# One slot size for the rest of a routed expert layer, and the count of slots read ahead of the last slot's work

## The chip, the core and the metric

The kernel runs on one core of a Trainium2 chip. Its engines are TensorE (PE in the profile; PEld is its weight load), VectorE (DVE), ScalarE (ACT), GpSimd (POOL) and SyncE (SP, which issues most DMAs). A name with a q behind it (POOLq) is that engine's sequencer. The metric is the device time of one execution in microseconds.

## What is computed

Attention of 8 batches and 8 heads over 576 positions of 64 values, in which every score below the row's maximum less tau is dropped; then a layer of 8 experts, in which each of the 4608 tokens goes to the one expert with the highest gate.

```python
def _attn_ref(q, k, v, tau):
    scores = np.matmul(q, k.transpose(0, 1, 3, 2)) / np.sqrt(q.shape[-1])
    thresh = np.max(scores, axis=-1, keepdims=True) - tau
    scores = np.where(scores >= thresh, scores, -1000000000.0)
    attn = np.exp(scores - np.max(scores, axis=-1, keepdims=True))
    return np.matmul(attn / (np.sum(attn, axis=-1, keepdims=True) + 1e-09), v)

def _moe_ref(x, modality_id, w_gate, modality_bias, w1, w2):   # x: 4608 x 512
    logits = x @ w_gate + modality_bias[modality_id]           # 8 experts
    e_idx = np.argmax(logits, axis=1)
    probs = np.exp(logits - logits.max(-1, keepdims=True))
    gate_w = (probs / (probs.sum(-1, keepdims=True) + 1e-09))[np.arange(N), e_idx]
    for e in range(E):
        mask = e_idx == e
        out[mask] = gate_w[mask, None] * (np.maximum(x[mask] @ w1[e], 0.0) @ w2[e])
    return out
```

## The kernel before

The attention runs in 288 steps, one tile of 128 rows of scores each. Every matrix is held as a high and a low part (names that end in h and l), and a product is three matmuls, so TensorE works nearly without a pause.

The expert layer is worked in **slots**: a slot is one expert and up to 512 rows of tokens (`slot`). Each token's row number and gate weight is scattered into a DRAM table `tab` (line 683), sorted by expert; the table is first filled with a row number that no token has (`fill`, line 259). A slot reads which expert it is (`expert`, line 795) and where its rows lie in the table (`rows`, line 799) into SP's registers, loads that piece of the table (`tb`, line 801) and its weights (lines 838 and 842), gathers the tokens' rows `xg` with an indirect DMA on POOL (line 814), transposes them on TensorE (line 828) into `xh` and `xl`, multiplies by w1 (line 874, result through `hh` on ACT, line 885, and `hl` on DVE, line 886) and by w2 (line 901), adds up the two halves (`y0` on ACT, line 909; `y` on DVE, line 914), and scatters the finished rows to the output with an indirect DMA on POOL (line 916). Weights are split into high parts on ACT (line 856) and low parts on POOL or DVE (line 860).

Seven **side slots** (256, 384, 512, 512, 512, 448 and 512 rows) are worked among the attention's steps. What is then left is planned once by `pick_rest`, a run of small operations on one partition of DVE that ends in the table `si` (the experts, the row offsets, and the number of slots). Before the change it plans with three slot sizes, 512, 384 and 256 rows. Three **tail slots** of 512 rows always follow (`ALWAYS`). Behind them stand conditional slots, for routings that need more: `ask` (line 1126) reads one number, `more_i`, into a register of every engine, and each engine tests it (line 1211) and jumps over the conditional code where it is zero. In the profiled execution it is: there are 37 gathers and 37 scatters of 128 rows, 25 of the side slots and 12 of the three tail slots.

An order written by hand by due times (`at`) sets when each piece is put into the program. Within the attention's steps PE and POOL keep it; the rest is placed by the scheduler. Instructions with the same issue order token (`tc.stamp_issue_order_token`) keep the order among themselves.

## Time and profile before

| | us |
|---|---|
| runs | 1012.5, 1012.56, 1022.66 (median 1012.56) |
| the profiled execution | 1011.88 |
| its span, first to last record | 1010.2 |
| PE busy in the span | 986.6 (98%) |
| DVE, ACT, POOL busy | 681.3, 633.5, 524.8 |
| mean granted clock of TensorE | 0.998 |

The profiled execution is a run of its own, beside the three timed ones; 1.68 us of its time lie outside the span. Times in a trace count from the span's start. "Busy" leaves out what only a sequencer does (register reads, branches, semaphores, DMA issues). A chain of waits is followed back from the last instruction, at each step to what released it; "issue" in it is time for which no releaser shows.

### The profile page before, as it was taken

How to read it: one execution, taken by the hardware profiler on the slowest of the kernel's cores; microseconds unless marked ns; L12 is line 12 of the kernel's file. 1: busy time of each engine (PE TensorE's matmuls, PEld its weight loads, DVE VectorE, ACT ScalarE, POOL GpSimd, SP SyncE). 2: the span in 40 equal slices, each digit the busy share in tenths (PEclk: the TensorE clock that was granted, in tenths of full speed). 3: DMA queues.
4: the chain of work that ended last, by engine and by line, in shares of the span. 5: the costliest groups of instructions: out<-in, count | busy, mean ns of one | idle time of the engine just before them, and what ended most of it. 6: DMA issues, size and time to landing. Idle time of an engine off the chain costs nothing.

```text
span 1010.2 us, 20293 instructions
## 1 busy us (share of the span) xinstructions
PE 986.6 (98%) x6556; PEld 795.0 (79%) x6556; DVE 681.3 (67%) x1698; ACT 633.5 (63%) x1439; POOL 524.8 (52%) x728
## 2 busy tenths in 40 slices
PE   7999999999999999999999999999999999999996
PEld 6777777788888887788778888788878867888885
DVE  6888987778677766777677877777766764333422
ACT  6787887676676666666667666666667625334430
POOL 4363467377538553655455654646567274534311
PEclk9999999999999999999999999999999999999999
DMA  6667777679647665676647555667666227634301
GB/s 154 145 158 169 137 196 196 169 161 237 170 124 168 187 159 133 144 184 163 165 112 177 153 158 133 152 160 197 153 150 165 82 81 200 204 108 139 116 10 44
DMA packets 206803, 151.83 MB, mean 150 GB/s; under 512 B 100062, under 2 KB 167646, under 8 KB 206688
## 3 DMA queue, kind: packets, MB, share of 16 engines
q1 hardware_dynamic: 199488, 131.53, 53.0%
q0 software_dynamic: 7200, 18.92, 5.9%
q8 instruction: 54, 0.88, 0.4%
q14 instruction: 61, 0.50, 0.2%
HBM read 80.05 MB, written 19.48 MB: 99 GB/s over the span
## 4 chain that ended last, share of the span: by engine, by line
PE 74%; DVE 9%; issue 9%; DMA 2%; ACT 2%; POOL 2%; SPq 1%; POOLq 0%; DVEq 0%; ACTq 0%
PE bk L521 15%; PE s L402 14%; PE bk L487 10%; PE bk L901 10%; PE bk L874 10%; PE pm L901 4%; PE pm L874 3%; DVE pr L459 2%; DVE nm L435 2%; PE bk L339 2%; PE bk L828 2%; PE bk L512 1%; PE bk L573 1%; ACT e L445 1%; DMA xg<-xs,tb 1%
## 5 line engine op out<-in xcount | busy, mean ns | idle before, releaser
L435 DVE TENSOR_REDUCE nm<-s 128x1 f32<-128x576 f32 x254 | 190.9, 752 | 97.4 <-PE s L402 95.3
L459 DVE SCALAR_TENSOR_TENSOR pr<-s,nm,e 128x576 f32<-128x576 f32 x254 | 204.8, 815 | 62.7 <-ACT e L445 58.9
L445 ACT ACTIVATE e<-s,nm 128x576 f32<-128x576 f32 x254 | 188.6, 743 | 59.5 <-DVE nm L435 52.6
L402 PE MATMUL s<-km,q 128*128 128x288 f32 x1024 | 196.5, 313 | 7.5 <-DVE pr L459 6.4
L497 ACT COPY ptm<-bk 128x512 f32<-128x512 f32 x256 | 149.4, 584 | 53.2 <-PE bk L487 52.6
L487 PE MATMUL bk<-ident,pr 128*128 128x128 f32 x1152 | 173.8, 273 | 0.0
L402 PEld LDWEIGHTS s<-km,q 128*128 128x128 f32 x1024 | 146.3, 189 | 24.5 <-DVE pr L459 18.2
L487 PEld LDWEIGHTS bk<-ident,pr 128*128 128x128 f32 x1152 | 140.6, 140 | 27.3 <-issue 6.2
L521 PE MATMUL bk<-ptm,v_m 128*64 128x320 f32 (+1 forms) x1024 | 140.7, 412 | 0.3 <-DVE hl L886 0.3
L860 POOL TENSOR_TENSOR w2l<-raw,w2h 128x512 fp32r<-128x512 f32 x77 | 98.5, 1287 | 32.6 <-ACT w2h L856 28.6
L521 PEld LDWEIGHTS bk<-ptm,v_m 128*64 128x64 f32 x1024 | 68.2, 136 | 50.8 <-issue 7.9
L916 POOL DMA_INDIRECT out_dram<-y,tb x37 | 38.0, 1026 | 122.2 <-DVE y L914 92.2
L476 ACT COPY rp<-pr 128x64 f32<-128x64 f32 x271 | 60.0, 248 | 43.8 <-DVE pr L459 41.5
L874 PE MATMUL bk<-xh,w1h 128*128 128x512 f32 (+3 forms) x204 | 82.1, 402 | 0.1
L313 POOL CAST nk<-str 128x64 fp32r<-128x64 f32 x31 | 7.4, 240 | 138.3 <-ACT str L327 130.9
L874 PE MATMUL bk<-xl,w1h 128*128 128x512 f32 (+3 forms) x204 | 74.2, 363 | 0.0
L874 PE MATMUL bk<-xh,w1l 128*128 128x512 f32 (+3 forms) x204 | 74.1, 363 | 0.0
L901 PE MATMUL bk<-w2h,hh 128*128 128x512 f32 x168 | 73.4, 437 | 0.0
L860 POOL TENSOR_TENSOR w1l<-raw,w1h 128x512 fp32r<-128x512 f32 x53 | 68.1, 1285 | 4.2
L901 PE MATMUL bk<-w2h,hl 128*128 128x512 f32 x168 | 66.2, 394 | 0.0
L901 PE MATMUL bk<-w2l,hh 128*128 128x512 f32 x168 | 66.1, 393 | 0.0
L814 POOL DMA_INDIRECT xg<-xs,tb x37 | 39.0, 1053 | 38.4 <-DMA tb<-tab 16.5
(211 smaller groups left out, 1973.6 us busy)
## 6 DMA issues: line engine op xcount, KB each, us to landing
raw<-in_moe_w_dram SPq DMA_DIRECT2D x160, 256.0 KB, 3.5
q<-nq SPq DMA_DIRECT2D x124, 256.0 KB, 4.4
km<-nk SPq DMA_DIRECT2D x124, 144.0 KB, 2.5
v_m<-in_v_dram SPq DMA_DIRECT2D x32, 256.0 KB, 3.7
xs<-xr SPq DMA_DIRECT2D x32, 256.0 KB, 3.0
k_m<-in_k_dram SPq DMA_DIRECT2D x62, 128.0 KB, 3.2
q_m<-in_q_dram SPq DMA_DIRECT2D x62, 128.0 KB, 3.7
vr<-in_v_dram SPq DMA_DIRECT2D x64, 16.0 KB, 4.1
```

Of the source, the lines that this page charges most:

```text
L402: nc.tensor.matmul(out=sps[:, hf, 0:SH], lhsT=a, rhs=x, start=(z == 0), stop=(z == len(passes) - 1))
L435: in_line(nc.vector.tensor_reduce(out=nm[:, 0:1], in_=sv, axis=AX.XY, op=ALU.max, negate=True), two)
L445: in_line(nc.scalar.activation(out=e, in_=sv, func=AF.Exp, bias=nm[:, 0:1]), two and n < LEAD)
L459: in_line(nc.vector.scalar_tensor_tensor(out=pr.rearrange("p (a x) -> p a x", a=2), in0=s2[n % 2][:, :, 0:SH], scalar=th, in1=e, op0=ALU.i ...
L476: (nc.gpsimd.tensor_copy if 2 <= n < 46 else nc.scalar.copy)(out=state[("rp", p)][:, 2 * c + s + x, :], in_=pr[:, SA:S])
L487: nc.tensor.transpose(out=ps[:, kc * P:(kc + 1) * P], in_=pr[:, kc * P:(kc + 1) * P], identity=ident)
L497: in_line(nc.scalar.copy(out=ptm[:, s, :, (c % 2) * P:(c % 2 + 1) * P], in_=pv), n + 2 < LEAD)
L521: nc.tensor.matmul(out=o, lhsT=lhsT, rhs=rhs, start=start, stop=stop, skip_group_check=True)
L814: nc.gpsimd.indirect_dma_start(out=xg, out_offset=None, in_=xs[0:nrow, :], in_offset=bass.IndirectOffsetOnAxis(ap=box["tb"][:, t, 0:1].bit ...
L860: then(eng.tensor_tensor(out=lo, in0=raw, in1=hi.bitcast(F32), op=ALU.subtract), eng is nc.vector and (lined or late))
L874: nc.tensor.matmul(out=ps[:, 0:WT], lhsT=a[:, cs], rhs=x[:, c, :], start=(c == 0 and z == 0), stop=(c == KC - 1 and z == 2))
L901: nc.tensor.matmul(out=ps, lhsT=h[:, ts], rhs=w, start=(z == 0 and y == 0), stop=(z == F2 - 1 and y == 2))
```

## The change

It has five parts.

1. `pick_rest` plans with one slot size, 512 rows. The arrays with a dimension of three sizes lose it, the list of possible slots grows from 10 to 16, and `more_f`, `more_s`, `more_i` and `cnt` are gone. `si` holds the count of slots in its last place.
2. The table gets one more 512-row stretch for each expert (`TROWS` 37888 to 41984), and its fill is two DMAs from one tile of half the size.
3. In a slot whose last tile has 64 rows (the 448-row side slot), the gather, `y0`, `y` and the scatter touch 64 partitions.
4. `ask` reads the count from `si`, and its reads, one per engine, carry a token "asked", as do the first operations of the last always-run slot on each engine (`ends`): each engine's read then stands ahead of those.
5. After the last slot there is a nest of tests of that register (`more`), and no copy `done_y`.

```diff
-    CAP = -(-N // W) * W
-    NCH = CAP // W
+    NCH = -(-N // W)
+    CAP = (NCH + 1) * W
     TROWS = NE * CAP + 2 * W
...
-    MAXN = ((N - NE * (WM + 1)) // W + NE if N >= NE * (WM + 1) else N // (WM + 1),
...
-    ALWAYS = (-(-left_ // W), 0, 0)
-    MAXC = max(MAXN)
...
+    WR = W
+    MAXC = (N - NE) // WR + NE
+    ALWAYS = -(-max(W, N - sum(w for w, _ in SIDE)) // W)
...
                                         in1=mid_f[:, m, :].unsqueeze(2).to_broadcast(shp), op=ALU.mult)
             nc.gpsimd.tensor_tensor(out=bias_t, in0=bias_t, in1=bias_u, op=ALU.add)
 
-        fill = work.tile([P, TROWS // P, 2], I32, name="fill", tag="xr", bufs=2)
+        half = TROWS // P // 2
+        fill = work.tile([P, half, 2], I32, name="fill", tag="xr", bufs=2)
         nc.gpsimd.memset(fill[:, :, 0], N)
         nc.gpsimd.memset(fill[:, :, 1], 0)
-        nc.sync.dma_start(out=tab.rearrange("(p r) c -> p r c", p=P), in_=fill)
+        for y in range(2):
+            nc.sync.dma_start(out=tab[y * half * P:(y + 1) * half * P, :].rearrange("(p r) c -> p r c", p=P), in_=fill)
         return bias
 
 
...
-        for z, w in enumerate((WM, WH, 0)):
...
-        for z in range(3):
...
+        th = fin["xp"].tile([1, NE, NCH], F32, name="th", bufs=1)
+        nc.vector.tensor_tensor(out=th, in0=th_lo, in1=left.unsqueeze(2).to_broadcast([1, NE, NCH]), op=ALU.is_lt)
+        ns = fin["xp"].tile([1, NE], F32, name="ns", bufs=1)
+        nc.vector.tensor_reduce(out=ns, in_=th, axis=AX.X, op=ALU.add)
+        cum = fin["xp"].tile([1, NE], F32, name="cum", bufs=1)
+        t = fin["xp"].tile([1, NE, NE], F32, name="cum_t", bufs=1)
+        nc.vector.tensor_tensor(out=t, in0=ns.unsqueeze(1).to_broadcast([1, NE, NE]), in1=tri, op=ALU.mult)
+        nc.vector.tensor_reduce(out=cum, in_=t, axis=AX.X, op=ALU.add)
...
-        for z in range(3):
...
+        le = fin["xp"].tile(SHP, F32, name="le", bufs=1)
+        nc.vector.tensor_tensor(out=le, in0=ij.unsqueeze(2).to_broadcast(SHP),
+                                in1=cum.unsqueeze(1).to_broadcast(SHP), op=ALU.is_ge)
+        ej = fin["xp"].tile([1, MAXC], F32, name="ej", bufs=1)
...
+        si = glob.tile([1, 2 * MAXC + 1], I32, name="si")
+        nc.vector.tensor_scalar(out=si[:, 0:MAXC], in0=ej, scalar1=float(NE - 1), scalar2=None, op0=ALU.min)
+
+        off = fin["xp"].tile([1, NE], F32, name="off", bufs=1)
+        nc.vector.tensor_tensor(out=off, in0=cum, in1=ns, op=ALU.subtract)
+        nc.vector.tensor_scalar(out=off, in0=off, scalar1=float(-WR), scalar2=None, op0=ALU.mult)
+        nc.vector.scalar_tensor_tensor(out=off, in0=taken, scalar=float(U), in1=off, op0=ALU.mult, op1=ALU.add)
+        em = fin["xp"].tile([1, MAXC], F32, name="em", bufs=1)
...
-        for z in range(3):
...
+        nc.vector.tensor_tensor(out=le, in0=em.unsqueeze(2).to_broadcast(SHP),
+                                in1=iota_m[0:1, :].unsqueeze(1).to_broadcast(SHP), op=ALU.is_equal)
+        nc.vector.tensor_tensor(out=le, in0=le, in1=off.unsqueeze(1).to_broadcast(SHP), op=ALU.mult)
+        bj = fin["xp"].tile([1, MAXC], F32, name="bj", bufs=1)
...
+        nc.vector.scalar_tensor_tensor(out=bj, in0=ij, scalar=float(WR), in1=bj, op0=ALU.mult, op1=ALU.add)
...
-        nc.vector.tensor_scalar(out=si[:, :, 0:MAXC], in0=ej, scalar1=float(NE - 1), scalar2=None, op0=ALU.min)
-        nc.vector.tensor_scalar(out=si[:, :, MAXC:2 * MAXC], in0=bj, scalar1=float(W + NE * CAP), scalar2=None,
...
-        nc.vector.tensor_copy(out=si[:, :, 2 * MAXC:], in_=cum[:, :, NE - 1:NE])
...
-        for z in range(3):
-            nc.vector.tensor_scalar(out=more_f[:, z], in0=cum[:, z, NE - 1:NE], scalar1=float(-ALWAYS[z]), scalar2=0.0,
...
-        nc.vector.tensor_reduce(out=more_s, in_=more_f.rearrange("a z o -> a (z o)"), axis=AX.X, op=ALU.add)
...
-        nc.vector.tensor_copy(out=more_i, in_=more_s)
...
+        nc.vector.tensor_scalar(out=si[:, MAXC:2 * MAXC], in0=bj, scalar1=float(W), scalar2=float(W + NE * CAP),
+                                op0=ALU.add, op1=ALU.min)
+        nc.vector.tensor_copy(out=si[:, 2 * MAXC:], in_=cum[:, NE - 1:NE])
         return si
...
+                w = TP(t)
...
+                    out=xg[0:w], out_offset=None, in_=xs[0:nrow, :],
...
+                part = eng.tensor_tensor(out=lo, in0=raw, in1=hi.bitcast(F32), op=ALU.subtract)
+                then(part, eng is nc.vector and (lined or late))
+                asked(part, ends and (which, f_) == (2, FC - 1))
...
+                    asked(nc.tensor.matmul(out=ps[:, 0:WT], lhsT=a[:, cs], rhs=x[:, c, :],
+                                           start=(c == 0 and z == 0), stop=(c == KC - 1 and z == 2)),
+                          ends and f_ + c + z == 0)
...
+                    asked(nc.scalar.activation(out=hh[:, 0:WT], in_=ps[:, 0:WT], func=AF.Relu), ends and f_ == 0)
+                    asked(nc.vector.scalar_tensor_tensor(out=hl[:, 0:WT], in0=ps[:, 0:WT], scalar=0.0,
+                                                         in1=hh[:, 0:WT].bitcast(F32), op0=ALU.max, op1=ALU.subtract),
+                          ends and f_ == 0)
...
                     lambda which, f_: nc.vector if which == 1 else nc.gpsimd, (lambda: fin["xp"], (2, 4)),
-                    lined=z + j == 0, pack=2 * SIZES[z] == W)
+                    lined=j == 0, ends=j == ALWAYS - 1)
 
     fin = {}
...
     at(XF, finish)
 
+    def asked(i, on=True):
+
+        if on:
+            tc.stamp_issue_order_token(_inst(i), "asked")
+
     def ask():
-        fin["more"] = nc.values_load(fin["more_i"][0:1, 0:1], min_val=0, max_val=sum(MAXN))
+        reads, (fin["more"],) = nc.values_load_multi_w_load_instructions(
+            fin["si"][0:1, 2 * MAXC:], min_val=0, max_val=MAXC)
+        for i in reads:
+            asked(i)
     at(F0 + C['ask'], ask)
     t0 = F0
...
         at(NSTEP + LAG + z / 2, f)
     run_events(0, 10 ** 9)
 
-    def more(cnt, j, z):
-        if j < MAXN[z]:
+    def more(cnt, j):
+        if j < MAXC:
             with tc.If(cnt > j):
-                for e in sorted(sum(last_slot(j, z), []), key=lambda x: x[0]):
+                for e in sorted(sum(last_slot(j), []), key=lambda x: x[0]):
                     e[1]()
-                more(cnt, j + 1, z)
-
-    done_y = tiny.tile([1, 1], F32, name="done_y", bufs=1)
-    nc.scalar.copy(out=done_y, in_=fin["y"][0:1, 0:1])
-    with tc.If(fin["more"] > 0):
-        for z in range(3):
-            m = nc.values_load(fin["si"][0:1, z, 2 * MAXC:], min_val=0, max_val=MAXN[z])
-            more(m, ALWAYS[z], z)
+                more(cnt, j + 1)
+
+    more(fin["more"], ALWAYS)
```

How the instructions stand on an engine changes in these places; otherwise PE, ACT and POOL keep their order up to the branch. A row has its number on its engine, the line in that kernel's file, the operation, and the semaphores that it waits for (DMASW and DMAHW are DMA queues).

POOL at the end of the program before: five scatters of finished rows (the first belongs to the second tail slot, the others to the last), the register read, the branch.

```order
695 L916 DMA out_dram<-y,tb 4608x512 [waits DMASW5_49,DVE_49]
696 L916 DMA out_dram<-y,tb 4608x512 [waits DMASW6_49,DVE_49]
697 L916 DMA out_dram<-y,tb 4608x512 [waits DMASW7_49,DVE_49]
698 L916 DMA out_dram<-y,tb 4608x512 [waits DMASW0_49,DVE_49]
699 L916 DMA out_dram<-y,tb 4608x512 [waits DMASW1_49,DVE_49]
700 L1126 TENSOR_LOAD more_i [waits DVE_49]
701 L1211 COMPARE_AND_BRANCH
```

And now, from three pieces of weights ahead of them:

```order
692 L836 TENSOR_TENSOR w2l<-raw,w2h 128x512 [waits DMAHW2_49,Activation_49]
693 L1107 TENSOR_LOAD si [waits DVE_49]
694 L836 TENSOR_TENSOR w2l<-raw,w2h 128x512 [waits DMAHW4_49,Activation_49]
695 L893 DMA out_dram<-y,tb 4608x512 [waits DMASW5_49,DVE_49]
696 L893 DMA out_dram<-y,tb 4608x512 [waits DMASW6_49,DVE_49]
697 L893 DMA out_dram<-y,tb 4608x512 [waits DMASW7_49,DVE_49]
698 L893 DMA out_dram<-y,tb 4608x512 [waits DMASW0_49,DVE_49]
699 L893 DMA out_dram<-y,tb 4608x512 [waits DMASW1_49,DVE_49]
700 L1188 COMPARE_AND_BRANCH
```

The read has gone from behind the last scatter to ahead of the last piece of w2's low part; behind the last scatter stands the branch alone. On DVE and ACT the read has moved in the same way, from behind the last `y` (on ACT from behind `done_y`, which is gone) to ahead of the last slot's first `hl` and `hh`.

PE at the end of the program before: the last matmuls, the read, the branch.

```order
3842 L901 MATMUL pm<-w2h,hl 128x512
3843 L901 MATMUL pm<-w2h,hh 128x512
3844 L901 MATMUL pm<-w2l,hh 128x512
3845 L901 MATMUL pm<-w2h,hl 128x512
3846 L1126 TENSOR_LOAD more_i [waits DVE_49]
3847 L1211 COMPARE_AND_BRANCH
```

And now, at the start of the last tail slot (the three matmuls by w2 are still the slot's before it):

```order
3652 L878 MATMUL pm<-w2h,hh 128x512
3653 L878 MATMUL pm<-w2l,hh 128x512
3654 L878 MATMUL pm<-w2h,hl 128x512
3655 L1107 TENSOR_LOAD si [waits DVE_49]
3656 L851 MATMUL pm<-xh,w1h 128x512 [waits DVE_49,Activation_49]
3657 L851 MATMUL pm<-xh,w1h 128x512 [waits DVE_49] x2
3658 L851 MATMUL pm<-xl,w1h 128x512 [waits DVE_49]
```

The read has moved ahead of the last slot's first matmul by w1, which waits for `xh` (ACT) and `xl` (DVE); 192 matmuls are now behind it.

SP before, where it goes from the last side slot's weights to the first tail slot: the load of a w2 piece, the reads of the experts (line 795) with the read of `more_i` among them, and the next loads. ISA rows are the steps of a register read or of an address.

```order
880 L842 DMA raw<-in_moe_w_dram 128x512 [waits DMAHW6_49,DMAHW0_49,Pool_49]
881 L795 TENSOR_LOAD si [waits DVE_49]
882 L795 ISA x2
883 L1126 TENSOR_LOAD more_i [waits DVE_49]
884 L1126 ISA x2
885 L795 TENSOR_LOAD si
886 L795 ISA x2
887 L795 TENSOR_LOAD si
888 L795 ISA x2
889 L842 ISA
890 L842 DMA raw<-in_moe_w_dram 128x512 [waits DMAHW1_49,DVE_49,Activation_49]
```

And now, two rows behind the read of the count (line 1107), which has become the first of these:

```order
882 L818 ISA
883 L818 DMA raw<-in_moe_w_dram 128x512 [waits DMAHW7_49,DMAHW1_49,Pool_49]
884 L818 ISA
885 L818 DMA raw<-in_moe_w_dram 128x512 [waits DMAHW2_49,DVE_49]
886 L770 TENSOR_LOAD si [waits DVE_49]
887 L770 ISA x2
888 L770 TENSOR_LOAD si
889 L770 ISA x2
890 L774 TENSOR_LOAD si [waits DVE_49]
891 L774 ISA x2
892 L770 TENSOR_LOAD si
893 L770 ISA x2
```

The count is read ahead of the w2 loads; a second w2 load (row 885) has moved ahead of the reads; the first slot's row offset (line 774, before line 799, row 903, behind four loads of w1 and three of w2) is read among the experts. Behind it come the same loads and then the load of `tb`.

On DVE the plan is 20 small operations instead of 36, among the same `hl` and `w1l`; `si`'s count is written after the 7th of them.

## Rows read from the trace of the kernel before

**Rows 1.** Page part 1, busy time, share of the span and instructions of the matmul engine

```profile
PE 986.6 (98%) x6556; PEld 795.0 (79%) x6556; DVE 681.3 (67%) x1698; ACT 633.5 (63%) x1439; POOL 524.8 (52%) x728
```

**Rows 2.** Waits of PE from 820 to 1002 us: total, times, longest

```profile
PE bk L521 <- DVE oh L656: 1.4, 1, 1.4
PE bk L828 <- DMA xg<-xs,tb: 0.5, 1, 0.5
```

**Rows 3.** Window: us, busy us (xinstructions) of five engines, granted clock, DMA share, GB/s

```profile
840.00:845.00 5.00, 5.00 (x24) 4.14 (x23) 0.78 (x2) 2.00 (x4) 0.00 (x0) 1.00 1.10 323
```

**Rows 4.** Chain of waits, end of the kernel: start us, us, what

```profile
1001.26 3.23 issue
1004.48 0.51 POOLq L1126
```

**Rows 5.** Timeline, same stretch: start, us, engine, line [idle before <-releaser]

```profile
999.26 0.75 DVE L914 SCALAR_TENSOR_TENSOR y<-pm,tb,y 128x512 f32<-128x512 f32 x1 [2.00 <-PE pm L901]
...
1000.28 0.97 POOL L916 DMA_INDIRECT out_dram<-y,tb  x1 [1.77 <-DVE y L914]
...
1002.19 0.75 DVE L914 SCALAR_TENSOR_TENSOR y<-pm,tb,y 128x512 f32<-128x512 f32 x1 [2.18 <-PEq L1211]
...
1004.69 0.98 POOL L916 DMA_INDIRECT out_dram<-y,tb  x1 [3.44 <-issue]
```

**Rows 6.** Scatters of line 916, 990 to 1001 us: durations min/median/max, landings

```profile
L916 POOL DMA_INDIRECT out_dram<-y,tb x3: 971/972/983, 994.8 to 1000.3; - x3
...
DMA to landing us min/median/max: 2.7/2.7/2.7
```

**Rows 7.** Register reads of line 1126, duration ns, first and last start

```profile
L1126 PEldq TENSOR_LOAD <-more_i x1: 483/483/483, 997.7 to 997.7; - x1
...
L1126 POOLq TENSOR_LOAD <-more_i x1: 509/509/509, 1004.5 to 1004.5; - x1
```

**Rows 8.** Branch of line 1211 and what follows it, same columns

```profile
L1211 POOLq EVENT_SEMAPHORE  x6: 17/30/43, 1007.7 to 1008.1; - x6
...
L1211 POOLq COMPARE_BRANCH  x1: 53/53/53, 1005.1 to 1005.1; - x1
L1211 POOLq INC_SWDGE_SEM  x1: 348/348/348, 1008.2 to 1008.2; - x1
```

**Rows 9.** Waits of SP's queue, 1000 to 1011 us

```profile
SPq L1241 <- DMA out_dram<-y,tb: 57.8, 1, 57.8
```

**Rows 10.** Timeline of DVE, 823 to 836 us, three steps of the plan

```profile
828.81 0.15 DVE L760 CAST si<-cum 1x3 int32<-1x3 f32 x1
...
832.71 1.39 DVE L753 TENSOR_TENSOR bj<-bj,ij 1x30 f32<-1x30 f32 x1
...
835.03 0.17 DVE L758 TENSOR_SCALAR si<-bj 1x30 int32<-1x30 f32 x1
```

**Rows 11.** Waits of SP's queue, 826 to 846 us

```profile
SPq L842 <- POOL w1l L860: 9.1, 1, 9.1
```

**Rows 12.** Timeline of SP's DMA issues, 826 to 850 us

```profile
834.07 3.94 SPq L842 DMA_DIRECT2D raw<-in_moe_w_dram  x3
```

**Rows 13.** Chain of waits ahead of the first tail slot

```profile
840.79 1.59 SPq L842
843.56 3.81 DMA tb<-tab
...
848.17 4.78 DMA xg<-xs,tb
```

**Rows 14.** Timeline, PE at the last tail slot's first matmul

```profile
957.90 0.54 PEld L874 LDWEIGHTS pm<-xh,w1h 128*128 128x128 f32 x3 [0.54 <-ACT xh L303]
```

**Rows 15.** Line 874, 953 to 959 us: PE's sequencer at that matmul

```profile
L874 PEldq EVENT_SEMAPHORE  x1: 51/51/51, 954.5 to 954.5; - x1
```

**Rows 16.** Line 259, the fill of the table, duration ns, start

```profile
L259 SPq DMA_DIRECT2D tab<-fill x1: 537/537/537, 56.0 to 56.0; - x1
```

**Rows 17.** Waits of PE from 50 to 80 us

```profile
PE s L402 <- DVE pr L459: 0.3, 1, 0.3
```

More of the change, by code (lines that the diff above doesn't have):

```diff
@@ L194, in tile_attn_moe @@
                             base=0, pattern=[[1, NE], [-1, NE]], channel_multiplier=0)
-    cnt = glob.tile([1, 4, NE], F32, name="cnt")
-    nc.gpsimd.memset(cnt[:, 0], 0.0)
     pay = glob.tile([P, B, NT, 2], I32, name="pay")
@@ L724, in pick_rest @@
-        ns = fin["xp"].tile([1, 3, NE], F32, name="ns", bufs=1)
-        nc.vector.tensor_tensor(out=ns, in0=cnt[:, 1:4, :], in1=cnt[:, 0:3, :], op=ALU.subtract)
-        off = fin["xp"].tile([1, 3, NE], F32, name="off", bufs=1)
-        nc.vector.scalar_tensor_tensor(out=off, in0=taken.unsqueeze(1).to_broadcast([1, 3, NE]),
-                                       scalar=float(U) / W, in1=cnt[:, 0:3, :], op0=ALU.mult, op1=ALU.add)
-        cum = fin["xp"].tile([1, 3, NE], F32, name="cum", bufs=1)
@@ L746, in pick_rest @@
-        for z in range(3):
-            nc.vector.tensor_tensor(out=le[:, z], in0=em[:, z].unsqueeze(2).to_broadcast(SHP),
-                                    in1=iota_m[0:1, :].unsqueeze(1).to_broadcast(SHP), op=ALU.is_equal)
-            nc.vector.tensor_tensor(out=le[:, z], in0=le[:, z], in1=off[:, z:z + 1, :].to_broadcast(SHP),
-                                    op=ALU.mult)
-        bj = fin["xp"].tile([1, 3, MAXC], F32, name="bj", bufs=1)
+        th = fin["xp"].tile([1, NE, NCH], F32, name="th", bufs=1)
@@ L778, in then, with slot @@
             tc.stamp_issue_order_token(_inst(i), "weights")
-    def slot(where, group, nrow, WT=W, wq=lambda: wp, nbuf=(4, 3, 5), lo_eng=None, xq=None, late=(), lined=False, pack=False):
+    def slot(where, group, nrow, WT=W, wq=lambda: wp, nbuf=(4, 3, 5), lo_eng=None, xq=None, late=(), lined=False, ends=False):
         ev, pe, xts = [], [], []
@@ L878, in f @@
                     let_go(ps)
-                    if not pack or f_ % 2 == 0:
-                        box["hp"] = [xp.tile([P, W], F32R, name=nm, bufs=F2) for nm in ("hh", "hl")]
-                    hh, hl = [t[:, (f_ % 2) * WT:] for t in box["hp"]] if pack else box["hp"]
+                    hh, hl = [xp.tile([P, W], F32R, name=nm, bufs=F2) for nm in ("hh", "hl")]
                     if WT % P:
```

78 lines of the change are left out of this document (20 added, 58 removed).

## The prediction

> **What bounds the kernel now.** I read the page's busy times first: PE works 986.6 us of a span of 1010.2, 98% [rows 1]. So I looked only for places where PE stands still and the change touches them, and for the stretch behind PE's last matmul. The list of PE's waits over the whole part in which the rest is planned and worked, 820 to 1002 us, has two entries [rows 2]: 1.4 us in the last routing step, which the change leaves alone, and 0.5 us in which the first tail slot's transposes wait for the gathered rows `xg`. Everything else that the change shortens there lies beside a busy PE. Behind PE's last matmul, about 1002.2 us, the span goes on for 8.0 us. The chain of waits through that end [rows 4] runs over POOL: 3.23 us without a releaser, then POOL's register read (line 1126), then the last scatter. SP ends the program and waits 57.8 us for that scatter's landing [rows 9]. So two places can give time: 8 us at the end, and 0.5 us ahead of the first tail slot.
>
> **The end.** The timeline [rows 5] shows what is odd there. A `y` that starts at 999.26 and takes 0.75 ends at 1000.01, and its scatter starts at 1000.28, 0.27 us later. The last `y` ends at 1002.19 + 0.75 = 1002.94, but its scatter starts only at 1004.69, 1.75 us later. That is 1.48 us too many, and the row names no releaser. The only difference in POOL's order is what stands behind it: behind the earlier ones another scatter, behind the last one the register read and the branch. In the trace the read starts at 1004.5, takes 0.509 us [rows 7], and so begins before the scatter that precedes it in the program. I take the 1.48 us as belonging to this read, since nothing else is new there. That it is the read, and not the branch behind it, is my choice; the rivals have the other case.
>
> What the end consists of from there: the scatter lands 2.7 us after its start, as the three ahead of it do [rows 6], which for the last one would be 1007.39. POOL's branch runs at 1005.1, and the next event of POOL's stream comes at 1007.7, 2.6 us later; six of these events go to 1008.1, and then comes the instruction that waits for the scatters, at 1008.2 [rows 8]. From there to the span's end, 1010.2, are 2.0 us of closing semaphores on all engines, which the change does not touch. So the landing was over by 1008.2 at the latest, 3.5 us after the scatter's start, and at the earliest after 2.7.
>
> With the read far ahead (the order puts it before the last piece of w2's low part, so POOL passes it long before the last scatters), the scatter starts at 1002.94 + 0.27 = 1003.21. It lands between 1003.21 + 2.7 = 1005.9 and 1003.21 + 3.5 = 1006.7. The branch now follows the scatter at once, at 1003.2 to 1003.3; 2.6 us later, 1005.9, POOL goes on, and with 0.5 us for its six events it stands at its wait at 1006.4. The wait ends at 1006.4 to 1006.7 instead of 1008.2: 1.5 to 1.8 us less, and I take 1.6. DVE's read and ACT's `done_y`, read and branch also leave the end, but both engines are done before POOL, so they count nothing.
>
> The Trainium skill (Runtime: NRT & Kernel Launch, "Instruction fetch mechanics") says that a taken branch whose target is outside the fetched window makes the engine wait for a fetch of its instructions before it goes on. The 2.6 us between POOL's branch and its next event [rows 8] agree with that; by this rule the 2.6 us stay in the changed kernel, since a branch is still taken, and only their start moves, which is how the sum above has it.
>
> **The reads at their new places.** On PE the read stands ahead of the last slot's first matmul by w1. A read takes PE's sequencer 0.483 us [rows 7]. That matmul starts at 957.90 and its weight load has waited 0.54 us for `xh` from ACT [rows 14], while PE's sequencer had come to it at 954.5 [rows 15], 3.4 us before. So the read fits into that wait and costs 0; if the sequencer came later than 0.48 us before the matmul, it would cost at most 0.48. Queued behind it are the last slot's 192 matmuls by w1 and w2, which all go to the end. On POOL it stands ahead of the last split, and what follows is the four scatters at the end; on DVE and ACT it stands ahead of the first `hl` and `hh`, which wait for PE anyway. I put all of them at 0, with 0.48 as the upper bound.
>
> The Trainium skill (DMA: Bandwidth & Descriptors, "Latency and other measured facts") gives about 600 ns as the least that such a register load takes; the trace has 483 to 509 ns [rows 7], and the measurement decides. By the page the upper bound would be 0.6 instead of 0.48, and the sum the same.
>
> **The plan and SP's queue.** The plan's last result, the row offsets in `si`, is written at 835.03 + 0.17 = 835.20 [rows 10]. Now 16 of its 36 operations go. At 0.15 to 0.2 us each (most rows of the plan are like the 0.15 and 0.17 shown) that is some 3 us of DVE, with `bj` by `ij`, 1.39 us, shortened too [rows 10]. DVE is not what PE waits for there. SP gets to these results late anyway: its w2 load waited 9.1 us for POOL [rows 11] and went out at 834.07 [rows 12]. The read of the count, now ahead of that load, needs the count that before was written at 828.81 + 0.15 [rows 10] and lies 5 us inside that wait: 0. Behind it the order has the same loads, with the row offset's read before them instead of behind. So `tb`'s load can be issued earlier, by at most the 1.1 us for which SP's reads had stood waiting for the offset (834.07 to 835.20). But it does not wait for its issue alone: a load's issue ahead of it was held for 1.59 us at 840.79, and `tb` then took 3.81 us [rows 13] behind loads of 256 KB, at a DMA share of 1.10 and 323 GB/s [rows 3]. The bytes ahead of it are the same. The gain lies between 0 and the whole 0.5 us of PE's wait [rows 2]; I take 0, because `tb` stands in a full queue.
>
> **The rest.** The second fill DMA costs SP one more issue, 0.537 us at 56 us [rows 16]. PE waits 0.3 us in all from 50 to 80 us, and for DVE [rows 17], so loads are far enough ahead to hide it; without that cover it would be 0.54. A 64-row last tile in one side slot saves some rows of one gather and one scatter beside a busy PE: 0. The copy `done_y` and POOL's memset of `cnt` go: 0. The larger table is touched only where rows are written. The three tail slots stay three, and the nest of conditional slots is jumped over by one branch as before.
>
> **Sum.** 1.6 us at the end, 0 elsewhere. The profiled execution took 1011.88 (span 1010.2 and 1.68 outside it), which becomes 1010.3. The median of the runs shown is 1012.56, 0.68 above that execution, so I forecast 1012.56 - 1.6 = 1011.0.
>
> **Rivals.**
>
> *The delay stays (0.25).* The 1.48 us belong to something else at the program's end: the branch that still follows the scatter, or the fetch of code around it. For it: the row names no releaser. Against it: DVE's last `y` has a branch behind it too and starts without such a gap, 2.93 us after the one before [rows 5] (it has a read behind it as well, so this speaks only weakly). Then the scatter still starts at 1004.7 and lands by 1008.2, and the time is that of before, 1012.6.
>
> *The end gains and the tail starts earlier too (0.15).* The offset's read ahead of the loads brings `tb` and `xg` 0.5 us forward: another 0.5 off, 1010.5. The queue at 1.10 speaks against it.
>
> *The row offset is late (0.05).* SP now reads it ahead of the four w1 loads, and they, `tb` and the gather stand behind that read. SP comes to it after two loads and two expert reads, about 836 us. Before, the offset was there at 835.20. If the new plan wrote it later than 836, each us would move the first tail slot by one, and PE with it: from 1.6 us late on, at 837.6, the whole gain is gone, and at 839 the time would be 1014. 16 operations fewer speak against it.
>
> *The reads are not covered (0.05).* PE's, 0.48, adds to the case in which the delay stays: 1013.1.
>
> *The change gains more than the chain shows (0.02),* or something unforeseen in the attention part costs more than 10 us (0.03), where the trace shows no operation that changes.
>
> **The numbers.** The forecast has 0.45, the rest as above. From 1010.5 less 1.0 for the spread of the bounds and of runs to 1013.1 these hold over 8 in 10: 1009.3 to 1013.2. Faster or slower by over 1%, 10 us, about what a measurement of this kernel can tell from no change, needs one of the last two cases: 0.02 and 0.04; within 1%: 0.94.
>
> **What would show it.** Right: the last scatter starts about 0.3 us after the last `y` ends, POOL's stream goes on 2.6 us behind its branch, and the stretch behind the last `y` is shorter by 1.5 to 1.8 us; the wait for `xg` still there; no read ahead of PE's matmul with an idle PE behind it. Wrong: a last scatter that still starts 1.7 us after its `y`; a new wait of SP for the plan at line 774; a PE that waits at the last slot's first matmul for longer than before.

## The result: 1.2% slower, most of it in a stretch without work

| | before | changed |
|---|---|---|
| median of 6 runs each, us | 1015.96 | 1027.88 |
| lowest and highest | 1012.5, 1022.66 | 1026.35, 1033.31 |
| ratio, 95% interval | | 1.0122 [1.0100, 1.0144] |
| profiled execution, us | 1011.88 | 1026.35 |
| its span | 1010.2 | 1024.6 |
| end of the last `y` in it | 1002.94 | 1008.23 |
| from there to the span's end | 7.26 | 16.37 |

PE is busy 1.5 us longer than in [rows 1]; its share falls because the span is longer. The page's first part, changed kernel:

```profile
PE 988.1 (96%) x6556; PEld 795.1 (78%) x6556; DVE 676.8 (66%) x1679; ACT 634.0 (62%) x1438; POOL 524.1 (51%) x727
```

The 14.4 us between the two spans fall into two parts: the last `y` ends 5.3 us later, and 9.1 us more pass behind it. The end first. Timeline of the changed kernel (start, duration, engine, line):

```profile
1007.48 0.75 DVE L891 SCALAR_TENSOR_TENSOR y<-pm,tb,y 128x512 f32<-128x512 f32 x1 [2.03 <-PE pm L878]
1008.51 0.97 POOL L893 DMA_INDIRECT out_dram<-y,tb  x1 [1.81 <-DVE y L891]
```

The last `y` ends at 1007.48 + 0.75 = 1008.23 and the last scatter starts 0.28 us later; before it was 1.75 us [rows 5]. So the gain that was forecast for this place is there, 1.47 us. It is lost many times over in what follows. The branch and the instruction that waits for the scatters (lines 1188, 1211 before), and the closing drains (line 1220; count, then min/median/max in ns, first and last start):

```profile
L1188 POOLq COMPARE_BRANCH  x1: 53/53/53, 1008.3 to 1008.3; - x1
...
L1188 POOLq INC_SWDGE_SEM  x1: 2468/2468/2468, 1011.5 to 1011.5; - x1
```

```profile
L1220 POOLq DRAIN  x3: 40/107/9389, 1014.0 to 1024.0; - x3
```

INC_SWDGE_SEM took 348 ns before [rows 8] and takes 2468; the longest of the three drains takes 9389 ns, where before it took 732 (that row stands with experiment 4). Together 11.857 us against 1.080, 10.78 more. No engine has a record of work in that time, and no DMA packet moved from 1012 to 1024 us: POOL was held by something that the trace does not name.

Ahead of the last `y` PE waits at two places where it did not wait before (waits of PE, 50 to 150 us, changed kernel: total, times, longest):

```profile
PE s L398 <- DMA v_m<-in_v_dram: 2.0, 1, 2.0
...
PE bk L321 <- DMA kq_r<-in_q_dram: 1.0, 1, 1.0
```

By 140 us PE is 3.6 us later than before, 0.7 of it from before 110 us. Ahead of the tail the picture is that of [rows 2], with the wait for `xg` at 1.1 instead of 0.5 us:

```profile
PE bk L804 <- DMA xg<-xs,tb: 1.1, 1, 1.1
```

The rest is spread over the tail slots. In the second half of the last slot 48 matmuls by w2 follow each other without a pause; here are the first and the last of them, of the kernel before and of the changed one:

```profile
990.82 0.39 PE L901 MATMUL pm<-w2h,hh 128*128 128x512 f32 x1
...
1001.58 0.39 PE L901 MATMUL pm<-w2h,hl 128*128 128x512 f32 x1
```

```profile
996.12 0.40 PE L878 MATMUL pm<-w2h,hh 128*128 128x512 f32 x1
...
1007.05 0.40 PE L878 MATMUL pm<-w2h,hl 128*128 128x512 f32 x1
```

47 steps in 10.76 us are 0.2289 us for one; in 10.92 us (the starts shown are rounded) they are 0.2324. Over the tail's 288 such matmuls that is 1 us at most, less where other work lies between them, and every kernel with the same addresses shows the same pace, as will be seen. The granted clock is 1.00 in both.

### The profile page after: what moved, and what is told of

Same layout as the page of the kernel before. It is cut to its first block, busy times and chain, and to the rows that moved or that the text cites. A ratio compares the mean times of both kernels' runs of the same rounds, so it can differ in the third digit from the quotient of the medians.

```text
span 1024.6 us, 20269 instructions
## 1 busy us (share of the span) xinstructions
PE 988.1 (96%) x6556; PEld 795.1 (78%) x6556; DVE 676.8 (66%) x1679; ACT 634.0 (62%) x1438; POOL 524.1 (51%) x727
## 4 chain that ended last, share of the span: by engine, by line
PE 70%; issue 10%; DVE 7%; DMA 5%; POOL 3%; ACT 2%; SPq 1%; POOLq 0%; DVEq 0%; ACTq 0%
PE bk L517 14%; PE s L398 14%; PE bk L483 10%; PE bk L878 10%; PE bk L851 10%; PE pm L878 3%; PE pm L851 2%; PE bk L335 2%; DVE pr L455 2%; DVE nm L431 2%; DMA xg<-xs,tb 2%; PE bk L508 1%; DMA raw<-in_moe_w_dram 1%; PE bk L804 1%; POOL w2l L836 1%
## 5 line engine op out<-in xcount | busy, mean ns | idle before, releaser
L893 POOL DMA_INDIRECT out_dram<-y,tb x37 | 37.9, 1024 | 121.5 <-DVE y L891 94.9
L836 DVE TENSOR_TENSOR w1l<-raw,w1h 128x512 fp32r<-128x512 f32 x27 | 19.3, 720 | 60.4 <-ACT w1h L832 60.3
```

Source lines behind the costliest of these rows:

```text
L836: part = eng.tensor_tensor(out=lo, in0=raw, in1=hi.bitcast(F32), op=ALU.subtract)
L893: i = _inst(nc.gpsimd.indirect_dma_start(out=out, out_offset=bass.IndirectOffsetOnAxis(ap=tb[0:w, t, 0:1].bitcast(U32), axis=0), in_=y[0:w ...
```

## The experiments

The ratios are against runs of the kernel before on the same chip, taken between the others. Experiments 1 to 4 ran on one chip one after the other, 5 to 8 on a second and 9 to 12 on a third. The medians of the kernel before differ there: 1019.45, 1012.90 and 1013.94 us. So the ratios can be compared from one group to another, and the times cannot.

### 1. The reads back at the end

```diff
-    at(F0 + C['ask'], ask)
+    at(10 ** 8, ask)
...
-            tc.stamp_issue_order_token(_inst(i), "asked")
+            pass
```

> The changed kernel with one part undone: the engines read the count behind their last work again, as before (SP's read stays ahead of the w2 load). In the changed kernel POOL's closing drain took 9.39 us and the instruction ahead of it 2.47, where they took 0.73 and 0.35 before. Theory A (the branch that now follows the last scatter directly makes the drain long): the drain is back under 1 us, the last scatter starts 1.7 us after its y again, and the time falls by about 9 us to near 1018. Theory B (the 64-row tile changed what POOL's indirect DMAs leave behind) and theory C (something else, such as where the code lies): the drain stays near 9 us, and the time is that of the changed kernel or 1.5 us more.

Measured: 1032.29 us, ratio 1.0137 [1.0100, 1.0174]. The end (timeline; then the two closing instructions):

```profile
1012.45 0.75 DVE L891 SCALAR_TENSOR_TENSOR y<-pm,tb,y 128x512 f32<-128x512 f32 x1 [2.24 <-DMA out_dram<-y,tb]
1013.48 0.97 POOL L893 DMA_INDIRECT out_dram<-y,tb  x1 [2.01 <-DVE y L891]
```

```profile
L1187 POOLq INC_SWDGE_SEM  x1: 2468/2468/2468, 1017.3 to 1017.3; - x1
```

```profile
L1219 POOLq DRAIN  x3: 40/107/9389, 1019.8 to 1029.7; - x3
```

The register read stands behind the last scatter again, and the scatter still starts 0.28 us behind its `y` (1012.45 + 0.75 = 1013.20, and 1013.48). So the read does not delay it: the prediction's main step falls. Theory A falls too, the drain is unchanged.

### 2. 128 rows in the short tile

```diff
-                w = TP(t)
+                w = P
```

(at the gather and at `y0`, `y` and the scatter.)

> The changed kernel with one part undone: the last tile of the 448-row slot moves 128 rows in its gather and its scatter and y0 and y touch 128 partitions. Theory B: the drain at the end falls to under 1 us, 10 us less in all, near 1017. Theories A and C: no change, drain near 9 us, time within 2 us of the changed kernel.

Measured: 1021.24 us, ratio 1.0025 [1.0005, 1.0044].

```profile
1012.92 0.75 DVE L891 SCALAR_TENSOR_TENSOR y<-pm,tb,y 128x512 f32<-128x512 f32 x1 [2.03 <-PE pm L878]
1015.42 0.98 POOL L893 DMA_INDIRECT out_dram<-y,tb  x1 [3.28 <-issue]
```

```profile
L1188 POOLq INC_SWDGE_SEM  x1: 348/348/348, 1018.5 to 1018.5; - x1
```

```profile
L1220 POOLq DRAIN  x3: 40/107/732, 1018.9 to 1020.2; - x3
```

Both readings of before are back at once: the short end (0.348 and 0.732 us) and the late scatter (1.75 us behind its `y`), with the reads moved as in the changed kernel. So both hang on the two DMAs with 64 rows, which belong to the 448-row slot (its last gather and its last scatter, in the changed kernel's trace some 315 and 190 us ahead of the last scatter of all), and neither on the reads. That is theory B, and more than it said.

### 3. One fill DMA and the old table

```diff
-    CAP = (NCH + 1) * W
+    CAP = NCH * W
...
-        half = TROWS // P // 2
-        fill = work.tile([P, half, 2], I32, name="fill", tag="xr", bufs=2)
+        fill = work.tile([P, TROWS // P, 2], I32, name="fill", tag="xr", bufs=2)
...
-        for y in range(2):
-            nc.sync.dma_start(out=tab[y * half * P:(y + 1) * half * P, :].rearrange("(p r) c -> p r c", p=P), in_=fill)
+        nc.sync.dma_start(out=tab.rearrange("(p r) c -> p r c", p=P), in_=fill)
```

> The changed kernel with one part undone: the table has its old size and is filled by one DMA. In the changed kernel PE is 2.9 us later than before by 122 us and 3.6 us later by 140 us, with waits for loads (1.0 and 2.0 us) that the kernel before does not have. Theory D (the second fill DMA delays the loads behind it): these waits go, PE runs as before up to 140 us, the time falls by 3 us or more. Theory E (the difference is one of the chip or the run): the waits stay or come elsewhere, and the kernel before on the same chip shows them too. The drain at the end stays near 9 us under A and B.

Measured: 1031.03 us, ratio 1.0127 [1.0089, 1.0164], the ratio of the changed kernel. The fill is not what costs the 1%. Near 121 us PE waits 3.9 us here, longer than in the changed kernel's own trace, so the waits there come with one fill DMA too; whether the second one adds to them, this run can't tell.

### 4. The kernel before once more

> The kernel before as it is, for a trace on the same chip as the other three. Theory D: PE's waits between 50 and 150 us are those of its first trace (none for loads at 65 and 122 us), and the time is 1012 to 1013. Theory E: it has such waits here too, and the time is 1015 to 1016, as in its later runs (1015.88 to 1016.19). Its drain at the end is under 1 us under A and B; a drain of 9 us would make the end a matter of the chip too.

Measured: 1018.0 us, ratio 0.9991 [0.9970, 1.0011]; its closing drain takes 732 ns, as in its first trace. But PE's waits between 100 and 150 us are not those of the first trace, and the granted clock shows what follows such a wait (waits of PE; then windows: busy us of PE, PEld, DVE, ACT, POOL, granted clock, DMA share, GB/s):

```profile
PE s L402 <- DVE pr L459: 4.0, 1, 4.0
```

```profile
L1241 POOLq DRAIN  x3: 40/107/732, 1015.1 to 1016.4; - x3
```

```profile
121.00:123.00 2.00, 0.21 (x2) 0.00 (x0) 0.00 (x0) 0.49 (x1) 0.97 (x1) 1.00 0.83 109
123.00:125.00 2.00, 0.00 (x0) 0.00 (x0) 1.62 (x4) 0.77 (x2) 0.00 (x0) 0.53 0.81 137
125.00:127.00 2.00, 1.75 (x7) 1.73 (x8) 1.66 (x7) 0.98 (x4) 0.00 (x0) 0.50 0.64 149
127.00:129.00 2.00, 2.00 (x11) 1.98 (x10) 0.94 (x2) 1.23 (x2) 0.00 (x0) 0.50 0.58 134
...
131.00:133.00 2.00, 2.00 (x20) 2.00 (x19) 1.79 (x6) 2.00 (x6) 1.48 (x4) 1.00 0.34 76
```

PE stands nearly still from 121 to 125 us, and the granted clock goes from 1.00 to 0.50, that is 1.2 GHz, until past 129. PE is 5.8 us later than in the first trace by 130 us, 5.2 of it from this stretch, and the unchanged kernel lost this. The traces of experiments 1 to 4 all have a wait of 3.9 to 4.0 us there. So such a loss does not need the change: theory E. It is not shown that the change adds nothing. On the other two chips the step that starts at 151 us in the first trace comes 1.0 to 3.0 us later in the six kernels made from the changed one, and 0.3 and 1.0 us later in the two made from the kernel before. The whole time sets a limit to it: experiment 11, with the changed fill and plan, is as fast as the kernel before within 0.13%, 1.3 us. The trace with one more DMA (next) is 0.95 us late at 140 us and has the changed fill too.

### 5 to 7. One, two and forty more indirect DMAs

A count explains experiments 1 to 4: the kernel before has 114 indirect DMAs of 128 rows (40 scatters into the table, 37 gathers, 37 scatters of the output), and the late start comes at the 114th. With 9 places for each (128 rows over 16 DMA engines are 8, and one for the semaphore) that is 1026; the 114th DMA takes the places 1018 to 1026, across 1024. With two DMAs of 64 rows (5 places) the sum is 1018. To try it, POOL gets more DMAs, which move nothing that is used (shown for one; for two the first two batches have one each, for forty each batch has five):

```diff
     def scatter(b, posi):
+        for _ in range(int(b == 0)):
+            scr = small.tile([P, 16], F32, name="scr", bufs=5)
+            nc.gpsimd.indirect_dma_start(
+                out=scr, out_offset=None, in_=v.rearrange("b h s (x c) -> (b h s x) c", c=16)[0:N, :],
+                in_offset=bass.IndirectOffsetOnAxis(ap=pay[:, b, 0, 0:1].bitcast(U32), axis=0),
+                bounds_check=N - 1, oob_is_err=False)
```

> The changed kernel with one more indirect DMA on POOL (128 rows of an input into a scratch tile that nothing reads) ahead of the first batch's scatters. So far every kernel with 114 indirect DMAs of 128 rows each has a last scatter 1.5 us late and a closing drain of 0.73 us, and every kernel with 112 of them and two of 64 rows has a last scatter on time and a drain of 9.39 us. Theory R: POOL's DMA descriptors are written one behind the other into a store of fixed size, 9 places for a DMA of 128 rows in each of 16 rings (8 rows and one for the semaphore), 1024 places in all; 114 x 9 = 1026 comes round once, in the last scatter, 112 x 9 + 2 x 5 = 1018 does not; coming round costs the late start, not coming round the long end. With one more there are 1027: the last scatter is late by 1.5 us again, the end instruction takes 0.35 and the drain 0.73 us, and the time is 9 us below the changed kernel. Theory S (the 64-row form itself makes the drain long): drain 9.39 us, nothing else changes.

Measured: 1014.98 us, ratio 1.0017 [1.0005, 1.0029]. One useless DMA takes back nearly the whole loss of the change.

```profile
1003.19 0.75 DVE L897 SCALAR_TENSOR_TENSOR y<-pm,tb,y 128x512 f32<-128x512 f32 x1 [2.03 <-PE pm L884]
1005.70 0.98 POOL L899 DMA_INDIRECT out_dram<-y,tb  x1 [3.30 <-issue]
```

```profile
L1194 POOLq INC_SWDGE_SEM  x1: 348/348/348, 1008.9 to 1008.9; - x1
```

```profile
L1226 POOLq DRAIN  x3: 40/107/732, 1009.3 to 1010.9; - x3
```

Theory R in all three points: late by 1.76 us behind its `y`, 0.348, 0.732.

> As with one more indirect DMA, but two. Theory R: 1036 places, the store comes round in the scatter before the last: that one is late by 1.5 us and the last one on time (0.27 us behind its y), with a drain near 0.73 us. The time is then about 10.5 us below the changed kernel, 1.5 us below that with one more, and below the kernel before but for what the change costs elsewhere. Theory S: drain 9.39 us.

Measured: 1014.75 us, ratio 1.0021 [1.0008, 1.0034].

```profile
1002.66 0.75 DVE L897 SCALAR_TENSOR_TENSOR y<-pm,tb,y 128x512 f32<-128x512 f32 x1 [2.04 <-PE pm L884]
...
1005.17 0.98 POOL L899 DMA_INDIRECT out_dram<-y,tb  x1 [3.31 <-issue]
1005.44 0.75 DVE L897 SCALAR_TENSOR_TENSOR y<-pm,tb,y 128x512 f32<-128x512 f32 x1 [2.03 <-PE pm L884]
1006.47 0.97 POOL L899 DMA_INDIRECT out_dram<-y,tb  x1 [0.32 <-DVE y L897]
```

```profile
L1194 POOLq INC_SWDGE_SEM  x1: 368/368/368, 1009.8 to 1009.8; - x1
```

```profile
L1226 POOLq DRAIN  x3: 40/156/814, 1010.2 to 1012.1; - x3
```

As forecast, the scatter before the last is now the late one (1005.17 against an end of its `y` at 1003.41, 1.76 us) and the last one is on time (1006.19 and 1006.47). The time does not show the 1.5 us: in its trace the stretch from the last `y` to the end is 1.1 us shorter than with one DMA (6.2 instead of 7.3), but PE came 2.3 us later to it, 1.8 of it by 151 us, after the stretch near 122 us that differs between executions, and the intervals of the two ratios overlap.

> As with one more indirect DMA, but five for each batch, 40 in all; only the end is read, since the 40 cost POOL some 40 us on the way. Theory R in its first form (the end is long only where the store has not come round): drain 0.73 us. Theory R in its second form (the end is long in proportion to the place reached): 1018 + 360 - 1024 = 354 places of 1018 give 35% of the 10.8 us that the end instruction and the drain take beyond those of before, 3.7 us. Theory S: drain 9.39 us.

```profile
L1194 POOLq INC_SWDGE_SEM  x1: 1135/1135/1135, 1017.0 to 1017.0; - x1
```

```profile
L1226 POOLq DRAIN  x3: 40/107/3917, 1018.2 to 1022.7; - x3
```

Measured: 1.135 + 3.917 = 5.05 us, 3.97 more than the 1.08 of before; the second form said 3.7, the first 0 and theory S 10.8. The median of 1027.19 us holds POOL's 40 DMAs and says nothing else.

Here the count passes 1024 in the middle of the kernel. After the 64-row gather, the 96th, the 115th DMA takes the places 1023 to 1031; it is a gather too (timeline of POOL):

```profile
789.43 1.05 POOL L796 DMA_INDIRECT xg<-xs,tb  x1 [0.94 <-issue]
```

It starts after 0.94 us without a releaser. Wherever else in this trace POOL idles ahead of an indirect DMA and no releaser shows, it is 0.15 to 0.36 us. So the late start goes with the count and not with the end of the program, but it is 0.8 us here and not 1.5; why, no run shows.

So the closing time grows with the places written since the count last passed 1024:

| kernel | DMAs, places | places past the last 1024 | INC_SWDGE_SEM + drain, us |
|---|---|---|---|
| before, 128 rows again | 114, 1026 | 2 | 0.348 + 0.732 |
| one more | 115, 1027 | 3 | 0.348 + 0.732 |
| before with one more | 115, 1035 | 11 | 0.368 + 0.814 |
| two more | 116, 1036 | 12 | 0.368 + 0.814 |
| forty more | 154, 1378 | 354 | 1.135 + 3.917 |
| changed | 114, 1018 | 1018 | 2.468 + 9.389 |

From 354 to 1018 places it is 6.81 us more, 10.2 ns for a place; from 3 to 354, 3.97 us, 11.3 ns. The two numbers 9 and 1024 were taken to fit the first traces. From them it was forecast which scatter is late with 115 and 116 DMAs, and the 354 places; that the closing time goes by the place was one of two forms on record, and the other (long only where the count has not come round) has failed. The unit itself is not shown: 8 places for a DMA (4 for one of 64 rows) and 910 in all would fit the late starts as well. What the runs show is that the count comes round at the 114th DMA of 128 rows, that one of 64 rows counts for less than one of 128, and that the end is paid by what was counted since.

The Trainium skill (DMA: Bandwidth & Descriptors, "SWDGE vs HWDGE vs iDMA") says that for DMAs issued from GpSimd software writes a pair of descriptors for each DMA operation to rings in SBUF. A count that comes round is in line with that; that the places are such descriptors, no run here shows. What POOL does in the 9.4 us, and which piece of code it is, no trace here says either.

### 8. Addresses on multiples of 64 bytes

```diff
+    glob.tile([1, 8], F32, name="pad")
     tri = glob.tile([1, NE, NE], F32, name="tri")
```

> The changed kernel with a tile of 32 bytes more among the first ones in SBUF, so that all later tiles lie 32 bytes higher, on multiples of 64 bytes again as in the kernel before; in the changed kernel they lie 32 bytes beside one. In every trace with the changed addresses a matmul by w2 in the tail slots follows the one before after 0.2322 us, in both traces of the kernel before after 0.2289 us; matmuls by w1 take 0.227 us in all. Theory P (the addresses cost it): 0.2289 us, and 1 to 2 us less in all than the changed kernel. Theory Q (something else does): 0.2322 us. The drain stays at 9.39 us under both.

Measured: 1025.23 us, ratio 1.0115 [1.0093, 1.0138]. First and last of the 48 matmuls:

```profile
993.58 0.40 PE L879 MATMUL pm<-w2h,hh 128*128 128x512 f32 x1
...
1004.50 0.40 PE L879 MATMUL pm<-w2h,hl 128*128 128x512 f32 x1
```

10.92 us for 47 steps, 0.2324: unchanged. Theory P falls; it is not the address as such.

### 9. The short tile alone, in the kernel before

The gather, `y0`, `y` and the scatter of the kernel before take `[0:w]` with `w = TP(t)`, as in part 3 of the change, and nothing else changes.

> The kernel before with this one part of the change alone: the 448-row slot's last tile moves 64 rows in its gather and its scatter. Theory R (POOL's DMA descriptors fill a store of 1024 places for each of 16 rings, and the end costs some 10 ns for each place written since the store last came round: measured 1.08 us at 2 and 3 places, 1.18 at 12, 5.05 at 354, 11.86 at 1018): 1018 places, so end instruction and drain take 2.47 and 9.39 us, the last scatter is on time with the read still behind it, and the time is 9 us above the kernel before, near 1.009 of it. Theory S (it needs the changed kernel's code or its moved reads as well): drain 0.73 us, ratio 1.000.

Measured: 1022.07 us, ratio 1.0077 [1.0055, 1.0099].

```profile
1001.87 0.75 DVE L916 SCALAR_TENSOR_TENSOR y<-pm,tb,y 128x512 f32<-128x512 f32 x1 [2.00 <-PE pm L902]
...
1002.90 0.97 POOL L918 DMA_INDIRECT out_dram<-y,tb  x1 [1.78 <-DVE y L916]
```

```profile
L1213 POOLq INC_SWDGE_SEM  x1: 2468/2468/2468, 1006.6 to 1006.6; - x1
```

```profile
L1243 POOLq DRAIN  x3: 40/107/9389, 1009.1 to 1019.0; - x3
```

The whole effect in the old kernel: the last scatter on time with the read and the old branch behind it, 2.468 and 9.389 us at the end. 10.78 - 1.47 = 9.3 us was to be expected, and the interval says 5.6 to 10.0. So part 3 of the change, 64 rows fewer in two DMAs, made the change slow.

### 10. One more DMA, in the kernel before

The lines of experiment 5 (one scratch buffer instead of five) in the kernel before.

> The kernel before with one more indirect DMA of 128 rows into a scratch tile. Theory R: 1035 places, so the scatter before the last comes round and is 1.5 us late, the last one is on time (0.3 us behind its y, though the register read still stands behind it), the closing takes 1.2 us, and the end behind the last y is about 1 us shorter than in the kernel before. The first prediction's theory (the read behind the scatter delays it): the last scatter is 1.75 us behind its y.

Measured: 1011.52 us, ratio 0.9976 [0.9964, 0.9988].

```profile
1001.23 0.98 POOL L922 DMA_INDIRECT out_dram<-y,tb  x1 [3.25 <-issue]
1001.71 0.75 DVE L920 SCALAR_TENSOR_TENSOR y<-pm,tb,y 128x512 f32<-128x512 f32 x1 [2.23 <-PEq L1217]
...
1002.74 0.97 POOL L922 DMA_INDIRECT out_dram<-y,tb  x1 [0.53 <-DVE y L920]
```

The late start has gone to the scatter before the last, and the last one starts 0.28 us behind its `y` (1002.46, 1002.74). An added DMA, which does nothing, makes the kernel before 0.24% faster, 2.4 us with an interval of 1.2 to 3.6; its trace accounts for 0.8 of them behind the last `y` (6.4 us to the span's end instead of 7.3). The remaining 1.6 us are not explained. Its ratio is the lowest of all the kernels here.

### 11 and 12. The distance between the operands

In SBUF the tail's w2h and w2l lie in one pool, hh and hl in another; the pool between them (`xp2`) has lost 1728 bytes with the plan's arrays. The distance is counted from the first w2h to the first hh: 101440 bytes before, 99712 in the changed kernel. A tile in that pool sets the distance anew (432 values for the distance of before, 160 for one of 100352 bytes):

```diff
+        fin["xp"].tile([1, 432], F32, name="gap", bufs=1)
         fin["si"] = pick_rest()
```

> The changed kernel with one more indirect DMA (1027 places, a short end) and with a tile of 1728 bytes more in the pool ahead of the tail's weights, so that the weights w2h and w2l lie as far from hh and hl as in the kernel before (101440 bytes from w2h to hh; 99712 in the changed kernel, in the one with 32 bytes more among the first tiles too). Theory P2 (that distance sets the pace of the matmuls by w2): 0.2289 us from one to the next in the tail slots instead of 0.2322, 0.95 us over the 288 of them, and the time within 0.1% of the kernel before. Theory Q: 0.2322 us, and 0.17% above it as with one more DMA alone.

Measured: 1013.89 us, ratio 1.0000 [0.9987, 1.0013].

```profile
992.15 0.39 PE L884 MATMUL pm<-w2h,hh 128*128 128x512 f32 x1
...
1002.91 0.39 PE L884 MATMUL pm<-w2h,hl 128*128 128x512 f32 x1
```

10.76 us for 47 steps: 0.2289, as before. Both operands lie 288 bytes lower here than in the kernel before, so it is the distance that brings the pace back and not the place of one of them. With the DMA count past 1024 (1027 places, 0.348 and 0.732 us at the end) and the distance put right, the changed kernel is as fast as the kernel before, within 1.3 us either way: no more than that is left for all other parts of the change together.

> The changed kernel with two more indirect DMAs (1036 places) and a gap of 640 bytes, which makes the distance from w2h to hh 100352 bytes, a multiple of 2048, as it is from w1h to xh in every kernel here (49152), whose matmuls follow each other after 0.2270 us. Theory P2 in its full form: 0.2270 us for matmuls by w2 as well, 0.55 us less than in the kernel before over 288 of them; with the last scatter on time that is 1 to 1.5 us below the kernel before, ratio 0.9985 to 0.999. Theory Q: 0.2322 us and a ratio of 1.001.

Measured: 1013.84 us, ratio 0.9996 [0.9983, 1.0009].

```profile
991.19 0.39 PE L884 MATMUL pm<-w2h,hh 128*128 128x512 f32 x1
...
1001.84 0.39 PE L884 MATMUL pm<-w2h,hl 128*128 128x512 f32 x1
```

10.65 us for 47 steps: 0.2266, the pace of the matmuls by w1, 0.1 us per 47 below the kernel before. Theory P2 holds in its full form for the pace; over 288 matmuls it is 0.6 us at most, and the ratio can't tell that from 1: its expected 0.9985 to 0.9990 lies in the interval, and so does 1. The mechanism behind the distance stays open; the three distances say only that 101440 and 99712 bytes are slower than 100352 by 1.0% and 2.6%.

## Why the prediction was wrong

**The range.** 1009.3 to 1013.2 was forecast, faster by 1.6 us; it became slower by 1.2%. For slower by over 1% the text gave 0.04.

**The term that was missing.** "A 64-row last tile in one side slot saves some rows of one gather and one scatter beside a busy PE: 0." This step failed, and it is nearly the whole loss: 10.78 us more in POOL's two closing instructions (experiments 2 and 9). It was costed where it runs, beside a busy PE, and there it costs nothing. What it left behind for the end, nearly 1024 places written since the count last came round, was not in any row of before, since the kernel before closes at 2 places. The reads and the fill were given an upper bound (0.48 and 0.54 us); this term had none, and no rival names it.

**The end's gain: right in size by luck, wrong in its reason.** The last scatter was forecast at 0.27 us behind its `y`, and it is 0.28. But "I take the 1.48 us as belonging to this read" is wrong: with the read back behind the scatter the delay does not come (experiment 1), with the read far ahead and 128 rows it does (experiment 2). It goes with the DMA that takes the count across 1024, and it moves with the count from scatter to scatter (experiments 6 and 10). The changed kernel was spared it because its 64-row tile keeps the count at 1018, the same tile that costs the 10.78 us. The row [rows 4] named no releaser, and the read that stands next to it in the chain was taken for one. The rival "the delay stays" had the cause outside the read, which is right, and the outcome wrong.

**The branch.** Right but for 0.2 us: POOL's stream goes on at 1011.1, 2.8 us behind its branch at 1008.3 (2.6 before, [rows 8]).

**The reads at their new places.** Right, 0. PE's read lies at 959.6, 3.4 us ahead of the matmul that it precedes, and that matmul's weight load waits the same 0.54 us for `xh` as in [rows 14]:

```profile
L1107 PEldq TENSOR_LOAD <-si x1: 492/492/492, 959.6 to 959.6; - x1
L1107 POOLq TENSOR_LOAD <-si x1: 515/515/515, 962.5 to 962.5; - x1
```

```profile
963.02 0.53 PEld L851 LDWEIGHTS pm<-xh,w1h 128*128 128x128 f32 x3 [0.54 <-ACT xh L299]
```

**The plan and SP's queue.** Right to take 0. In the changed kernel the count's read waits 3.1 us for the plan, and the w2 load behind it waits 5.8 us more for POOL, as it waited 9.1 before [rows 11]; so the plan lies under that cover still (waits of SP's queue, 826 to 850 us):

```profile
SPq L818 <- POOL w1l L836: 5.8, 1, 5.8
SPq L1107 <- DVE off L732: 3.1, 1, 3.1
```

The wait for `xg` was 1.1 us here, 0.7 with 128 rows, none with one more DMA and none in the second trace of the kernel before. It varies between executions by as much as the 0.5 us that was to be won or lost, so nothing of the plan can be seen in the time. The rival "the row offset is late" did not come.

**The fill.** Nothing against 0: without the second fill DMA the ratio stays (experiment 3), though its interval, 0.89 to 1.64%, could not show half a microsecond.

**What no part of the sum had.** The plan's smaller arrays move the tail's weights by 1728 bytes against hh and hl, and 288 matmuls follow each other up to 1.5% more slowly, 1 us at most (experiments 8, 11, 12). The text looked at what instructions the change moves, and not at what addresses.

**The sum as it should have been**, from rows of the traces: -1.47 (scatter on time) + 10.78 (closing) + 1.0 at most (distance) = 10.3 us, 1.0%; the interval of the ratio is 1.0 to 1.4%. What lies between the two profiled spans beyond that, 4.1 us, is mostly there by 150 us. The unchanged kernel has lost more than that in the same stretch (experiment 4), and the change's own share of it is not shown; by experiment 11 it is 1.3 us at most.

## What to carry to other kernels

A row without a releaser is not explained by the instruction that stands beside it: before a gain is counted there, look for what is counted or filled up to that point (here DMAs issued from POOL since the start). Where a change alters how many rows POOL's DMAs move, in however cheap a place, compare the closing instructions of the kernel too, and try one DMA more or less; it takes 1 us beside other work, and here it took the ratio from 1.0122 to 1.0017 (each on a chip of its own, against the kernel before). And where tiles shrink or go, compare the pace of unchanged matmuls before and after, for it can change with the operands' places alone.

## What the hardware showed that was not expected

- POOL's closing instructions take 1.08 us or 11.86 us for the same work ahead of them, by how much its indirect DMAs have moved: counted as 9 places for 128 rows and 5 for 64, 10 to 11 ns for each place since the count last passed 1024 (the unit is fitted). Every kernel with the same count has the same times to the nanosecond.
- The DMA that takes the count across starts 1.5 us late near the end of a kernel (0.8 us in the one trace where it lies in the middle), and no row names what it waits for.
- Matmuls of the same shape follow each other after 0.2266, 0.2289 or 0.2324 us as the stationary and the moving operand lie 100352, 101440 or 99712 bytes apart, at a granted clock of 1.00 throughout.
- A stand of PE of 4 us at 121 us came with some 7 us at a granted clock of 0.50 (1.2 GHz), the first 2 of them within the stand, so that it cost 5.2 us in all. The two traces of the kernel before differ in this; they are of two executions.
